# Block-sparse attention and a gated product in one kernel: attention steps of 512 tokens instead of 256, the probabilities' detour through DRAM in nine transfers instead of eighteen, and the first unit transposed on TensorE

## The chip, the cores and the metric

The kernel runs on one core of a Trainium2 chip. That core has five engines with queues of their own: TensorE (PE, with its weight loads as PEld), VectorE (DVE), ScalarE (ACT), GpSimd (POOL) and SyncE (SP), which here only issues DMA transfers. Each engine works its queue strictly in order. The metric is the device time of one execution in microseconds (us).

## The reference: what is computed

Four sequences of 768 tokens go through attention with 8 heads of 64, and the result, 3072 tokens of 512, goes through a gated product.

```python
scores = scale * np.matmul(q, k.transpose(0, 1, 3, 2))
is_global = pos[None, :] < int(n_global)
is_local = (rel >= 0) & (rel < int(n_local))
keep = is_global | is_local
...
scores = scores + bias[None, :, :, :]
scores = np.where(keep, scores, -1000000000.0)
...
a = a / (np.sum(a, axis=-1, keepdims=True) + 1e-09)
return np.matmul(a, v).astype(np.float32)
...
a = x @ w_a
b = x @ w_b
return (a * b @ w_out).astype(np.float32)
```

A query sees the first 8 tokens and the 96 up to itself. The bias is a slope per head times the distance. The product's hidden size is 1536. All is float32.

## The kernel before

**Units and passes.** The 3072 tokens are six units of 512 (T, L38). The hidden columns are six groups of 256, two of which make a stage. `PASSES` (L47) names 18 passes: stage 0 over units 0 to 5, stage 1 back from 5 to 0, stage 2 from 0 to 5. A pass projects one unit's tokens with two groups (`project`, L811, whose seven products of 12 matmuls are L797 and go to the PSUM banks al and ga) and multiplies the gated result into four accumulators (`back`, L885, matmuls at L895, banks acc). Each float32 matmul is three of rounded parts: tokens (`forms`, L728) and weights (`wform`, L382) are split into a high part H and a low part L by a cast (L291 on ScalarE, L293 on VectorE) and a subtraction (L301). The seven products are a scheme of sums and differences, so that B11, T2 and the others are combinations of quarters of x, and A11, S2 and the others of quarters of the weights. A weight comes as 64-bit words (L322, 512 KB each) and is converted in steps on ScalarE (L328, L363) and VectorE (L335 to L370).

**Attention** of a unit must be done before its first pass. Unit 0's stands ahead of everything; the attention of unit u + 1 is spread over the second half of pass u - 1 or so and the first half of pass u. It is done in granules: one head pair (of four) and 256 tokens (NH = 2 blocks of 128), eight to a unit (`granule_ops`, L518).

- Loads: q in two transfers, one a head, into a buffer whose other half GpSimd set to zero once (L502), so that one matmul gives both heads' scores; keys kt and values vt, one transfer each.
- Scores: two matmuls a block (L555), of 168 columns each, for 64 queries of both heads and 168 keys. VectorE adds the mask and takes the maximum (L570), ScalarE does exp and the sum (L586), VectorE the reciprocal (L600, L605). The scaling of the granule goes to ScalarE in four instructions (L611) or to VectorE in one (L614), as the planner finds it.
- Turning: the values matmul needs the probabilities with the keys on the partitions. VectorE transposes blocks of 32 x 32 into tt (L624, L631). Four transfers write tt to a mirror in DRAM, mir, by 32 partitions each (L639). Five read it back with the blocks' rows in place: three into px (keys near the query block, and 8 lanes of global keys for each half), two into py (the others).
- Values: eight matmuls (L693) into the bank pa, half of a pair's 512 tokens. After the second granule pa is copied to x (L711).

**The order.** Nothing runs as it is written. Each step is recorded with a due time and a cost for each engine that may do it (`Schedule`, L121). A planner plays them through with those costs, lets the earliest due ready step go first, and writes out one fixed order per engine. A DMA counts as bytes / 330 ns, 90 ns at least, on one queue (L285). All transfers are issued by SyncE, in the planner's order: when one has to wait for a semaphore, all behind it wait. Buffers are tags with a number of copies (`TBUFS` and so on, L57 to L64); a step waits for a free copy. x takes two copies of a tag X, shared with the tokens that later passes load again (`load_x`, L776).

Of the kernel before, what the change touches and what calls it, by code (L numbers as in the profile page):

```python
# [12 lines left out]
F32 = mybir.dt.float32  # L13
# [12 lines left out]
P = 128  # L26
# [9 lines left out]
KB = KW + 72  # L36
# [6 lines left out]
NH = 2  # L43
# [22 lines left out]
AHEAD = 0.5  # L66
START = 44000.0
# [186 lines left out]
class Fast:  # L254
    def __init__(self, ctx, tc, a, out, nf):
        self.tc, self.nc = tc, tc.nc
        self.a, self.out, self.nf = a, out, nf
        self.ctx = ctx
        self.plan = Schedule()
        self.count = 0  # L260
        self.granule = 0

# [16 lines left out]
    def dma(self, due, out, src, reads, writes, nbytes):  # L279
        self.plan.op(  # L280
            due,
            lambda e: self.nc.sync.dma_start(out(), src()),  # L282
            reads,
            writes,
            dma=max(nbytes / 330.0, 90.0),  # L285
        )
# [23 lines left out]
    def to32(self, fp, piece, due, tag):  # L310
# [13 lines left out]
            dma=CN * 8 * P / 330.0,  # L324
# [67 lines left out]
    def convert(self, fp, due, step, direct):  # L392
# [19 lines left out]
        temp("S2", m["S1"], m["A11"], sub, t)  # L412
        self.wform(fp, "S2", t, m["S2"], direct)
        self.wform(fp, "S1", t + 200, m["S1"], direct)
        temp("S3", m["A11"], m["A21"], sub, t + 400, out=m["A21"])
# [4 lines left out]
        for f in range(2):  # L420
            w = self.to32(fp, 4 + f, due + (4 + f) * step, "mO")
            self.wform(fp, f"O{f}", due + (4 + f) * step, w, direct)
# [68 lines left out]
    def zeros(self):  # L491
        self.q = [self.sbuf([P, NH * 2, 2, 64], F32, f"q{i}", f"q{i}") for i in range(QBUFS)]
        self.px = [
            self.sbuf([104, 4, 2, NH, 32], F32, f"px{i}", f"px{i}") for i in range(PTBUFS)
        ]
        self.py = [self.sbuf([P, 4, 2, NH, 32], F32, f"py{i}", f"py{i}") for i in range(PTBUFS)]
        for q in self.q:
            for h in range(2):
                r = slice(64 * (1 - h), 64 * (1 - h) + 64)
                self.plan.op(  # L500
                    -1e6,
                    lambda e, q=q, r=r, h=h: self.nc.gpsimd.memset(q[r, :, h], 0.0),  # L502
                    [],
                    [(q, "z%d" % h)],
                    pool=400,
                )
# [11 lines left out]
    def granule_ops(self, u, p, hb, due, x):  # L518
        nc, op = self.nc, self.plan.op
        n = f"{u}_{p}_{hb}"  # L520
        g = self.granule
        self.granule += 1
        q, px, py = self.q[g % QBUFS], self.px[g % PTBUFS], self.py[g % PTBUFS]
        kt = self.sbuf([P, KN], F32, "kt", "kt" + n, KBUFS)
        vt = self.sbuf([P, VN], F32, "vt", "vt" + n, VBUFS)
        for h in range(2):
            r = slice(64 * h, 64 * h + 64)
            self.dma(
                due - LOADLEAD,
                lambda r=r, h=h: q[r, :, h],  # L530
                lambda h=h: self.a["qd"][u, p, hb, h].rearrange("d (s i) -> d s i", i=64),
                [],
                [(q, h)],
                64 * 1024,
            )
# [3 lines left out]
        self.dma(  # L539
            due + VLAG - 4000.0, lambda: vt[:, :], lambda: self.a["vd"][u, p, hb], [], [vt], VN * 4 * P  # L540
        )
        t = self.sbuf([P, NH, 2 * KW], F32, "t", "t" + n, TBUFS)
        sm = self.sbuf([P, 4, 2 * NH], F32, "sm", "sm" + n, 4)
        qreads = [(q, 0), (q, 1), (q, "z0"), (q, "z1")]
        for i in range(NH):
            blk = (4 * u + NH * hb + i) % NB
# [5 lines left out]
            def scores(e, i=i, ps=ps):  # L552
                for s in range(2):
                    k0 = i * KB + 72 * s
                    nc.tensor.matmul(  # L555
                        ps[:, s * KW : s * KW + KW],
                        q[:, 2 * i + s].rearrange("p h i -> p (h i)"),
                        kt[:, k0 : k0 + KW],
                        start=True,
                        stop=True,  # L560
                        skip_group_check=True,
                    )

            op(due, scores, qreads + [kt], [ps], pe=620)
# [33 lines left out]
        op(  # L598
            due,
            lambda e: nc.vector.tensor_scalar_add(sm[:, 2], sm[:, 1], 1e-9),  # L600
            [(sm, j) for j in range(4)],
            [(sm, "d")],
            dve=70,
        )
        op(due, lambda e: nc.vector.reciprocal(sm[:, 3], sm[:, 2]), [(sm, "d")], [(sm, "r")], dve=80)  # L605
        flat = lambda: t[:, :].rearrange("p a b -> p (a b)").rearrange("p (j k) -> p j k", k=KW)

        def norm(e):
            if e == "act":
                for j in range(2 * NH):  # L610
                    nc.scalar.mul(flat()[:, j], flat()[:, j], sm[:, 3, j : j + 1])  # L611
            else:
                r = sm[:, 3].rearrange("p (j o) -> p j o", o=1).to_broadcast([P, 2 * NH, KW])
                nc.vector.tensor_mul(flat(), flat(), r)  # L614

        ts = [(t, j) for j in range(4)]
        op(due, norm, [(sm, "r")], ts, port=BOTH, dve=dve(2 * NH * KW), act=4 * (act(KW) + 100))
        tt = self.sbuf([P, 2, 3, 2 * NH * 32], F32, "tt", "tt" + n, TTBUFS)

        def turn_x(e):  # L620
            src = t[:, :, 72:264].rearrange("p b (s e k) -> p b s e k", s=2, e=3)
            dst = tt[:, 0].rearrange("p e (s b k) -> p b s e k", b=NH, s=2)
            for i in range(NH):
                nc.vector.transpose(dst[:, i], src[:, i])  # L624

        def turn_y(e):
            for s in range(2):
                c = s * (2 * KW - 96)
                src = t[:, :, c : c + 96].rearrange("p b (e k) -> p b e k", e=3)
                dst = tt[:, 1].rearrange("p e (s b k) -> p s b e k", b=NH, s=2)  # L630
                nc.vector.transpose(dst[:, s], src)  # L631

        op(due, turn_x, ts, [(tt, 0)], dve=2 * dve(192))
        op(due, turn_y, ts, [(tt, 1)], dve=2 * dve(192))
        mir = self.dram([4, 2, 3, 32, P], F32, "mir" + n, "mir", 4)
        for k in range(4):
            self.dma(
                due,
                lambda k=k: mir[k].rearrange("a e j c -> j (a e) c"),  # L639
                lambda k=k: tt[32 * k : 32 * k + 32].rearrange("p a e c -> p (a e) c"),  # L640
                [(tt, 0), (tt, 1)],
                [(mir, k)],
                32 * 6 * 512 * 1.3,
            )
        ms = [(mir, k) for k in range(4)]

        def read(out, src, nbytes, writes):
            self.dma(due, out, src, ms, writes, nbytes)

        read(  # L650
            lambda: px[:96].rearrange("p g s b k -> p g (s b k)"),
            lambda: mir[:, 0].rearrange("g e j c -> (e j) g c"),
            96 * 4 * 512 * 1.3,
            [(px, "x")],
        )
        y = lambda: mir[:, 1].rearrange("g e j (s b k) -> s (e j) g b k", s=2, b=NH)
        read(
            lambda: py[:64, :, 0].rearrange("p g b k -> p g (b k)"),
            lambda: y()[0, :64].rearrange("p g b k -> p g (b k)"),
            64 * 4 * 256 * 2,  # L660
            [(py, 0)],
        )
        read(
            lambda: py[64:, :, 1].rearrange("p g b k -> p g (b k)"),
            lambda: y()[1, 32:96].rearrange("p g b k -> p g (b k)"),
            64 * 4 * 256 * 2,
            [(py, 1)],
        )
        for s, e0 in ((0, 64), (1, 24)):
            read(  # L670
                lambda s=s: px[96:104, :, s].rearrange("p g b k -> p g (b k)"),
                lambda s=s, e0=e0: y()[s, e0 : e0 + 8].rearrange("p g b k -> p g (b k)"),
                8 * 4 * 512,
                [(px, ("g", s))],
            )
        if hb == 0:
            tag = "psA" if u else FIRST["psA"][p % 2]
            self.pa = self.bank(tag, f"pa{u}_{p}")
        pa = self.pa

        def values(e):
            for i in range(NH):
                c0 = (NH * hb + i) * P
                v0 = i * 2 * P
                for c in range(2):
                    for h in range(2):
                        if c == 0:
                            rhs = px[:, 2 * h : 2 * h + 2, :, i].rearrange("p g s k -> p s g k")
                            lhs = vt[:104, v0 + 64 * h : v0 + 64 * h + 64]
                        else:  # L690
                            rhs = py[:, 2 * h : 2 * h + 2, :, i].rearrange("p g s k -> p s g k")
                            lhs = vt[:, v0 + P + 64 * h : v0 + P + 64 * h + 64]
                        nc.tensor.matmul(  # L693
                            pa[64 * h : 64 * h + 64, c0 : c0 + P],
                            lhs,
                            rhs,
# [6 lines left out]
        op(  # L703
            due + VLAG,
            values,
# [668 lines left out]
```

## Time and profile before

| what | us |
|---|---|
| median of three runs | 853.27 (852.32 to 854.04) |
| the profiled execution | 850.4 |
| its span, first to last instruction | 848.6 |
| TensorE busy in the span | 724.2 |
| VectorE busy | 580.0 |
| ScalarE busy | 378.1 |

The profile's page gives busy times, a chain of waits that ended last, and groups of instructions; the trace behind it can be asked for stretches of time. SPq is SyncE issuing transfers. A busy engine isn't one at its peak: matmuls overlap, and TensorE's clock is lowered at times (PEclk, 1.00 is full speed). DMA is the mean busy share of 16 transfer engines. In lists, names are line, engine, operation, and tiles as out<-in with buffer numbers left out; a time in a row's middle is the group's busy time, then the mean of one in ns.

### The profile page before, as it was taken

The numbers are of one execution on the slowest core, as the hardware profiler recorded it, in microseconds if no ns is written. First come the engines' busy times: TensorE is split into PE (matmuls) and PEld (weight loads), VectorE is DVE, ScalarE is ACT, GpSimd is POOL, SyncE is SP. The second block draws the span as 40 slices with busy tenths as digits, with TensorE's granted clock in tenths as the row PEclk, the third lists the DMA queues.
The fourth block names the chain that finished last, engine by engine and source line by source line (L and its number), as shares of the span: only waits on it lengthen the run. The fifth ranks groups of instructions, "written<-read, shape, count | busy, mean of one in ns | idle before, by whom it ended". The sixth has DMA issues, their size and how long they took to land.

```text
span 848.6 us, 14458 instructions
## 1 busy us (share of the span) xinstructions
PE 724.2 (85%) x5040; PEld 652.2 (77%) x5040; DVE 580.0 (68%) x1534; ACT 378.1 (45%) x952; POOL 2.7 (0%) x12
## 2 busy tenths in 40 slices
PE   3645778788888787888869999999999999999995
PEld 3544666577777576777669999999999999999994
DVE  5746977766668386477669988856765856765642
ACT  2644765735556464465446654323323322322320
POOL 1000000000000000000000000000000000000000
PEclk9855888789999999889979999999999999999998
DMA  6769688778878878889897666322353322420331
GB/s 191 193 162 280 203 206 221 209 186 227 219 198 238 251 225 217 202 229 241 240 333 240 215 225 222 121 91 99 131 162 101 102 80 73 149 88 13 100 100 66
DMA packets 162369, 149.60 MB, mean 176 GB/s; under 512 B 65392, under 2 KB 126832, under 8 KB 160240
## 3 DMA queue, kind: packets, MB, share of 16 engines
q1 hardware_dynamic: 162288, 148.59, 59.9%
q8 instruction: 42, 0.69, 0.3%
q14 instruction: 39, 0.32, 0.1%
HBM read 97.16 MB, written 51.38 MB: 175 GB/s over the span
## 4 chain that ended last, share of the span: by engine, by line
PE 57%; SPq 15%; DMA 13%; DVE 9%; issue 3%; ACT 2%; DVEq 0%; ACTq 0%
PE acc L895 19%; PE al L797 19%; SPq L282 14%; PE ga L797 14%; DMA px<-mir 4%; PE ps L555 3%; PE pa L693 2%; DMA wr<-wts 2%; DMA mir<-tt 2%; DMA kt<-kd 1%; DVE t L570 1%; ACT t L586 1%; DVE xT L301 1%; DVE s L826 1%; DVE tt L624 1%
## 5 line engine op out<-in xcount | busy, mean ns | idle before, releaser
L895 PE MATMUL acc<-w_O,hh 128*128 128x512 f32 x576 | 200.4, 407 | 0.9 <-ACT o L291 0.9
L895 PEld LDWEIGHTS acc<-w_O,hh 128*128 128x128 f32 x576 | 110.3, 192 | 25.3 <-ACT o L291 1.1
L555 PE MATMUL ps<-kt,q 128*128 128x168 f32 x384 | 88.4, 366 | 47.2 <-DMA kt<-kd 20.8
L797 PE MATMUL al<-xf_T,w_S 128*128 128x256 f32 x864 | 119.2, 288 | 5.9 <-ACT s L291 4.0
L797 PEld LDWEIGHTS al<-xf_T,w_S 128*128 128x128 f32 x864 | 111.2, 194 | 7.8 <-ACT s L291 4.8
L555 PEld LDWEIGHTS ps<-kt,q 128*128 128x128 f32 x384 | 69.7, 225 | 60.3 <-issue 24.4
L895 PE MATMUL acc<-w_O,hl 128*128 128x512 f32 x288 | 114.9, 399 | 0.5 <-DVE hl L301 0.5
L586 ACT ACTIVATE t<-t,sm 128x168 f32<-128x168 f32 x192 | 81.7, 427 | 71.3 <-DVE sm L570 65.9
L570 DVE CUSTOM_DVE_ANT_0 t<-ps,mask 128x168 f32<-128x168 f32 x192 | 57.0, 325 | 64.7 <-PE ps L555 64.3
L291 ACT COPY s<-al 128x512 f32<-128x512 f32 x70 | 41.0, 586 | 121.2 <-PE al L797 120.9
L693 PE MATMUL pa<-px,vt 104*64 104x128 f32 x384 | 47.1, 321 | 55.3 <-DMA px<-mir 32.8
L693 PEld LDWEIGHTS pa<-px,vt 104*64 104x64 f32 x384 | 27.0, 156 | 68.6 <-issue 31.0
L826 DVE TENSOR_TENSOR s<-ga,s 128x512 f32<-128x512 f32 x72 | 49.5, 688 | 39.0 <-PE ga L797 38.9
L291 ACT CAST hh<-h 128x512 fp32r<-128x512 f32 x62 | 38.2, 619 | 62.2 <-DVE h L301 36.5
L797 PE MATMUL ga<-xf_B,w_A 128*128 128x256 f32 x432 | 62.6, 295 | 2.6 <-DVE xf_B L301 1.5
L895 PEld LDWEIGHTS acc<-w_O,hl 128*128 128x128 f32 x288 | 55.3, 192 | 10.7 <-DVE hl L301 0.8
L797 PEld LDWEIGHTS ga<-xf_B,w_A 128*128 128x128 f32 x432 | 57.4, 200 | 4.3 <-DVE xf_B L301 2.3
L797 PE MATMUL ga<-xf_B,w_S 128*128 128x256 f32 x432 | 58.9, 286 | 1.7 <-ACT s L291 1.6
L797 PEld LDWEIGHTS al<-xf_B,w_A 128*128 128x128 f32 x432 | 57.6, 195 | 3.2 <-ACT t L611 0.3
L797 PE MATMUL al<-xf_B,w_A 128*128 128x256 f32 x432 | 59.8, 289 | 0.0
L797 PE MATMUL ga<-xf_T,w_S 128*128 128x256 f32 x432 | 57.9, 283 | 0.0
L797 PE MATMUL al<-xf_T,w_A 128*128 128x256 f32 x432 | 57.8, 283 | 0.1
(92 smaller groups left out, 1064.5 us busy)
## 6 DMA issues: line engine op xcount, KB each, us to landing
wr<-wts SPq DMA_DIRECT2D x36, 512.0 KB
mir<-tt SPq DMA_DIRECT2D x192, 96.0 KB
vt<-vd SPq DMA_DIRECT2D x48, 256.0 KB
kt<-kd SPq DMA_DIRECT2D x48, 240.0 KB
part<-o SPq DMA_DIRECT2D x40, 256.0 KB
xl<-dx SPq DMA_DIRECT2D x10, 1024.0 KB
o<-part SPq DMA_DIRECT2D x40, 256.0 KB
px<-mir SPq DMA_DIRECT2D x48, 192.0 KB
```

Of the source, the lines that this page charges most:

```text
L282: lambda e: self.nc.sync.dma_start(out(), src()),
L291: self.nc.scalar.copy(out(), src())
L301: lambda e: self.nc.vector.tensor_tensor(out(), a(), b(), op=op),
L555: nc.tensor.matmul(ps[:, s * KW : s * KW + KW], q[:, 2 * i + s].rearrange("p h i -> p (h i)"), kt[:, k0 : k0 + KW], start=True, stop=True, ...
L570: lambda e, i=i, w=w, ps=ps, j=j, kind=kind: nc.vector.tensor_tensor_reduce(t[:, i, w], ps[:, w], self.mask[p][:, kind, w], -0.125, 3.0e38 ...
L586: lambda e, i=i, w=w, j=j: nc.scalar.activation(t[:, i, w], t[:, i, w], AF.Exp, bias=sm[:, 0, j : j + 1], scale=-1.0, accum_out=sm[:, 1, j ...
L624: nc.vector.transpose(dst[:, i], src[:, i])
L693: nc.tensor.matmul(pa[64 * h : 64 * h + 64, c0 : c0 + P], lhs, rhs, start=c == 0, stop=c == 1, skip_group_check=True, tile_position=(0, 64 ...
L797: self.nc.tensor.matmul(bank[:, ab * HT : ab * HT + HT], w[:, a, (2 * ab + c) * P : (2 * ab + c) * P + P], x[:, b, c], start=first, stop=F ...
L826: lambda e: nc.vector.tensor_tensor(s[:, :], bank[:, :], s[:, :], op=ALU.add),
L895: self.nc.tensor.matmul(acc[i][:, :], a[:, rows], w[:, b], start=first and f == 0 and k == 0, stop=False, skip_group_check=True,)
```

## The change

A granule becomes one head pair and all 512 tokens of the unit (NH = 4). What follows from that and what is changed beside it:

- q and the keys come in one transfer, qk, of 7808 bytes for each of 128 partitions; q carries its zeros from DRAM. The keys are laid out once more, so that both halves of a block use overlapping windows (KB = KW + 64).
- Sums' reciprocals, scaling and transposes are done by halves of a granule (two blocks). On VectorE the scaling is four tensor_scalar instructions of 168 columns, no longer one multiplication with a broadcast.
- The mirror is written whole by one transfer, and read by eight: four into px of 32, 32, 32 and 8 partitions, four into py of 32 (`carry`).
- For unit 0 (`DIRECT`) there is no mirror. TensorE transposes each block's probabilities against an identity into PSUM (`direct`), and VectorE or ScalarE copies them to px and py. The identity is made ahead of the branch.
- px, py, tt and X have one copy each, K and V buffers two, temporaries s three. In bytes px, py, tt, t, qk and vt are twice as large as the granule's were.
- Due times of the start and the costs of the planner (DMA: bytes / 345, 340 ns at least, reads of the mirror at that least) are set anew, so the order shifts everywhere.

```diff
-KB = KW + 72
+KB = KW + 64
-NH = 2
+NH = 4
+QN = NH * 2 * P
...
+    "psT": ("acc3", "ga"),
...
-TTBUFS = 2
-PTBUFS = 2
-KBUFS = 3
-VBUFS = 3
-QBUFS = 2
-XBUFS = 2
+TTBUFS = 1
+PTBUFS = 1
+DIRECT = (0,)
+KBUFS = 2
+VBUFS = 2
+XBUFS = 1
...
-            dma=max(nbytes / 330.0, 90.0),
+            dma=max(nbytes / 345.0, 340.0),
...
         self.dma(
-            due - LOADLEAD, lambda: kt[:, :], lambda: self.a["kd"][u, p, hb], [], [kt], KN * 4 * P
+            due - LOADLEAD,
+            lambda: qk[:, :],
+            lambda: self.a["qk"][u, p],
+            [],
+            [qk],
+            (QN + KN) * 4 * P,
         )
...
-                r = sm[:, 3].rearrange("p (j o) -> p j o", o=1).to_broadcast([P, 2 * NH, KW])
-                nc.vector.tensor_mul(flat(), flat(), r)
+                    for j in js:
+                        nc.vector.tensor_scalar(
+                            flat()[:, j], flat()[:, j], sm[:, 3, j : j + 1], None, op0=ALU.mult
+                        )
...
+            if u in DIRECT:
+                for i in range(2 * half, 2 * half + 2):
+                    self.direct(u, n, i, due, t, px, py)
+                continue
...
+    def direct(self, u, n, i, due, t, px, py):
...
+        def turn(e):
+            for s in range(2):
+                x0, y0 = 64 + 104 * s, 272 * s
+                nc.tensor.transpose(
+                    bank[:104, s * P : s * P + P], t[:, i, x0 : x0 + 104], self.ident
+                )
+                nc.tensor.transpose(
+                    bank[:64, 256 + s * P : 256 + s * P + P], t[:, i, y0 : y0 + 64], self.ident
+                )
...
+    def carry(self, n, due, tt, px, py):
+        mir = self.dram([P, 6, 2 * NH * 32], F32, "mir" + n, "mir", 4)
+        self.dma(
+            due, lambda: mir[:, :], lambda: tt[:, :], [(tt, 0), (tt, 1)], [mir], 6 * 1024 * P
+        )
+        turned = lambda: mir[:, :].rearrange("(g j) e c -> j g e c", g=4)
+        for e in range(4):
+            lanes = 32 if e < 3 else NG
...
+                lambda e=e, lanes=lanes: turned()[:lanes, :, e],
+                [mir],
+                [(px, e)],
+                0,
+            )
...
-        temps = [self.sbuf([P, T], F32, "s", f"s{n}_{k}", 4) for k in range(3)]
+        temps = [self.sbuf([P, T], F32, "s", f"s{n}_{k}", 3) for k in range(3)]
...
-        x0 = self.attention(0, 0.0, START - 9000.0)
-        self.convert(0, START - 14000.0, 3000.0, True)
+        x0 = self.attention(0, 0.0, START - ATT0)
+        self.convert(0, START - CONV0, STEP0, True)
```

SyncE's queue before, at the first head pair of unit 1 (the digits after a name are unit, pair and granule half; 32x6x128 is partitions by runs by elements):

```order
L282 DMA mir1_0_0_807<-tt1_0_0_780 32x6x128 x4
L282 DMA q1_106<-qd 64x4x64 x2
L282 DMA kt1_2_0_838<-kd 128x480
L282 DMA px0_264<-mir1_0_0_807 96x4x128
L282 DMA py0_109<-mir1_0_0_807 64x4x64 x2
L282 DMA px0_264<-mir1_0_0_807 8x4x64 x2
L322 DMA wr1_2_872<-wts 128x512
L282 DMA mir1_0_1_881<-tt1_0_1_866 32x6x128 x4
L282 DMA q0_101<-qd 64x4x64 x2
L282 DMA kt1_2_1_911<-kd 128x480
L322 DMA wr1_3_935<-wts 128x512
L282 DMA px1_328<-mir1_0_1_881 96x4x128
```

The same place in SyncE's queue now:

```order
L290 DMA mir1_0_765<-tt1_0_720 128x1536
L330 DMA wr1_1_792<-wts 128x512
L290 DMA px0_214<-mir1_0_765 32x4x256 x3
L290 DMA px0_214<-mir1_0_765 8x4x256
L290 DMA py0_106<-mir1_0_765 32x4x128 x4
L290 DMA qk1_3_853<-qk 128x1952
L290 DMA vt1_2_911<-vd 128x1024
L290 DMA mir1_1_922<-tt1_1_843 128x1536
```

The write of the whole pair is one row and its reads eight issues; where the second granule's write and reads followed, the next pair's loads and its mirror stand.

TensorE's queue before, between the first and the second group of values matmuls of unit 0 (ps scores, pa values):

```order
L693 MATMUL pa0_0_304<-py0_109,vt0_0_0_132 64x128 x2
L555 MATMUL ps0_2_1_1_324<-kt0_2_1_206,q1_106 128x168 x2
L555 MATMUL ps0_3_0_0_331<-kt0_3_0_290,q0_101 128x168 x2
L555 MATMUL ps0_3_0_1_363<-kt0_3_0_290,q0_101 128x168 x2
L693 MATMUL pa0_0_304<-px1_328,vt0_0_1_137 64x128 x2
```

TensorE's queue now, at the same scores of unit 0's third pair (pt are the transposes; the two rows of a 64-query half have 104 and 64 columns of keys):

```order
L676 MATMUL pt0_0_3_228<-ident_60,t0_0_141 64x128
L544 MATMUL ps0_2_0_239<-qk0_2_166 128x168 x2
L544 MATMUL ps0_2_1_250<-qk0_2_166 128x168 x2
L673 MATMUL pt0_1_0_260<-ident_60,t0_1_169 104x128
L676 MATMUL pt0_1_0_260<-ident_60,t0_1_169 64x128
```

Four transposes a block now stand on TensorE in unit 0, where only scores and values stood, and a pair's values come in one group behind them.

More of the change, by code (lines that the diff above doesn't have):

```diff
@@ L261, in __init__ @@
         self.granule = 0
+        self.turns = 0
     def open(self):
@@ L645, in granule_ops @@
[L645 to L662, printed above, removed]
@@ L718, in granule_ops @@
                 psum=True,
             )
+    def carry(self, n, due, tt, px, py):
[6 more added lines that the diff above has]
+            lanes = 32 if e < 3 else NG
+            self.dma(
+                due,
+                lambda e=e, lanes=lanes: px[32 * e : 32 * e + lanes].rearrange(
+                    "p g s b k -> p g (s b k)"
+                ),
+                lambda e=e, lanes=lanes: turned()[:lanes, :, e],
[3 more added lines that the diff above has]
+            )
+        half = NH * 32
+        for s in range(2):
+            for e in range(2):
+                r = slice(64 * s + 32 * e, 64 * s + 32 * e + 32)
+                self.dma(
+                    due,
+                    lambda r=r, s=s: py[r, :, s].rearrange("p g b k -> p g (b k)"),
+                    lambda s=s, e=e: turned()[:, :, 4 + e, s * half : s * half + half],
+                    [mir],
+                    [(py, (s, e))],
+                    0,
+                )
```

290 lines of the change are left out of this document (129 added, 161 removed).

## The prediction, made before any run of the changed kernel

> **What bounds the kernel now.** I read the busy shares by stretch first, then the chain that ended last, then the DMA queue's own timeline. I cut the span at two instructions. At 85 us TensorE begins the product of S2 and T2, the first for which the weights and tokens of the first pass are really there. At 432 us the last values matmul of unit 5 is over, and attention with it. I call the pieces A (0 to 85), B (85 to 432) and C (432 to 848.6).
>
> ```profile
> core 0: us, PE busy (x) PEld busy (x) DVE busy (x) ACT busy (x) POOL busy (x), PEclk, DMA share, GB/s
> 0.00:85.00 85.00, 42.56 (x225) 36.36 (x226) 51.62 (x180) 38.10 (x115) 2.65 (x12) 0.72 0.75 206
> 85.00:432.00 347.00, 277.19 (x2022) 240.67 (x2021) 240.97 (x831) 194.95 (x582) 0.00 (x0) 0.92 0.82 222
> 432.00:520.00 88.00, 86.03 (x601) 80.63 (x601) 80.29 (x153) 50.85 (x93) 0.00 (x0) 0.97 0.74 249
> 520.00:840.00 320.00, 318.46 (x2197) 294.56 (x2195) 206.43 (x372) 94.18 (x165) 0.00 (x0) 1.00 0.31 102
> L797 PE MATMUL al<-xf_T,w_S x864: 276/280/582, 84.9 to 824.2; 128*128 128x256 f32 x173
> 428.33 1.99 PE pa L693 x16
> ```
>
> In C TensorE is busy throughout, at the full granted clock: 416.6 us that no DMA edit can shorten. In B it is busy for 277 us at a granted clock of 0.92, which is 277 x 0.92 = 255 us of work at full clock in 347 us. So 92 us of B are loss, and most of A is. The chain of waits, taken for B alone, says to what:
>
> ```profile
> by line: SPq L282 29.1%; DMA px<-mir 10.9%; PE ps L555 5.3%; PE pa L693 5.2%; issue 5.1%; PE acc L895 5.1%; DMA mir<-tt 4.5%; PE al L797 3.2%; DMA wr<-wts 2.9%; DMA kt<-kd 2.5%; DVE t L570 2.4%; PE ga L797 1.7%; ACT t L586 1.7%; DVE s L826
> ```
>
> The largest entry is neither a transfer nor an engine, but SyncE issuing transfers (SPq). Its timeline in B shows why: it issues without a pause.
>
> ```profile
> 276.20 0.32 SPq L282 DMA_DIRECT2D px<-mir  x1
> 276.58 1.26 SPq L282 DMA_DIRECT2D py<-mir  x2
> 277.88 0.85 SPq L282 DMA_DIRECT2D px<-mir  x2
> 278.83 0.34 SPq L282 DMA_DIRECT2D part<-o  x1
> 279.22 1.23 SPq L282 DMA_DIRECT2D q<-qd  x2
> 280.50 0.60 SPq L282 DMA_DIRECT2D kt<-kd  x1
> 281.21 2.11 SPq L282 DMA_DIRECT2D mir<-tt  x4
> 283.37 0.47 SPq L322 DMA_DIRECT2D wr<-wts  x1
> 283.89 0.44 SPq L282 DMA_DIRECT2D vt<-vd  x1
> ```
>
> From 276.20 to 284.33 the issues alone fill 7.62 of 8.13 us. Now per head pair and 512 tokens (two granules): q 4 x 0.61, kt 2 x 0.60, vt 2 x 0.44, mir 8 x 0.53, px 2 x 0.32, py 4 x 0.63, the small px 4 x 0.43 = 13.6 us. Some twenty pairs lie in B, 272 us of its 347. The 20 pairs' 26 issues each are what sets B's pace, with the DMA engines at 0.82 close behind.
>
> **What the change does to the queue.** A pair now issues one qk, one vt, one mirror write and eight reads, 11 in place of 26. None of these shapes is in the trace. The rows above lie between 0.32 (px) and 0.63 (py), so 11 issues cost between 3.5 and 6.9 us. I take 0.45, near wr and vt: 5.0 us, 100 us in B. SyncE stops being the bound, with room to spare at either end. What is late next has to be found among the engines.
>
> **DMA bytes in B.** The sizes now:
>
> ```profile
> mir<-tt SPq DMA_DIRECT2D x192, 96.0 KB
> vt<-vd SPq DMA_DIRECT2D x48, 256.0 KB
> kt<-kd SPq DMA_DIRECT2D x48, 240.0 KB
> px<-mir SPq DMA_DIRECT2D x48, 192.0 KB
> q<-qd SPq DMA_DIRECT2D x96, 64.0 KB
> py<-mir SPq DMA_DIRECT2D x96, 64.0 KB
> px<-mir SPq DMA_DIRECT2D x96, 8.0 KB
> DMA packets 162369, 149.60 MB, mean 176 GB/s; under 512 B 65392, under 2 KB 126832, under 8 KB 160240
> ```
>
> A pair moves 8 x 96 + 2 x 256 + 2 x 240 + 2 x 192 + 4 x 64 + 4 x 64 + 4 x 8 = 2688 KB. After: qk 976 (the zeros that GpSimd wrote into q are now loaded), vt 512, mirror 768, reads 3 x 128 + 32 + 4 x 64 = 672, together 2928 KB. So the bytes grow by 240 KB a pair; only the packets shrink in number. B moves 347 x 222 = 77 MB now and 77 + 20 x 0.246 = 82 MB then. What a byte costs depends on the packet, and the stretches show it: divided by their share, B carries 222 / 0.82 = 271 GB/s, the next two stretches 249 / 0.74 = 336 and 102 / 0.31 = 329. They move rows of 2 KB and more, B mostly pieces of 256 and 512 B. The new qk, vt and mirror write are rows of 4 to 8 KB, the reads are still 512 B and 1 KB. So I price the 20 x 0.69 = 14 MB of reads at 271 and the other 68 MB at 333: 51 + 204 = 255 us of DMA time, against 0.82 x 347 = 285 now. At the present rate for all of it, it would be 82 / 271 = 303.
>
> **VectorE and TensorE in B.**
>
> ```profile
> L624 DVE STREAM_TRANSPOSE tt<-t 128x192 f32<-128x192 f32 x96 | 30.8, 357 | 8.2 <-DMA mir<-tt 6.7 <-ACT t L586 0.8 <-ACT t L611 0.5
> L631 DVE STREAM_TRANSPOSE tt<-t 128x192 f32<-128x192 f32 x96 | 28.6, 337 | 0.0
> L614 DVE TENSOR_TENSOR t<-t,sm 128x672 f32<-128x672 f32 x15 | 12.8, 856 | 0.2
> L335 DVE TENSOR_SCALAR wm<-wm 128x512 f32<-128x512 f32 x36 | 15.3, 424 | 25.9 <-ACT wm L328 25.9
> L600 DVE TENSOR_SCALAR sm<-sm 128x4 f32<-128x4 f32 x48 | 7.9, 165 | 7.5 <-ACT t L586 7.3
> ```
>
> A pair's transposes stay eight instructions over 1536 columns in all (4 x 256 + 4 x 128 for 8 x 192): no change. The scaling becomes four tensor_scalar of 168 columns for a half. That shape isn't in the trace; it lies between 165 and 424 ns, and I take 200, by its length. VectorE gets 31 of the 48 halves, some 96 such instructions in B: 19 us for about 12 x 0.856 = 10. VectorE goes from 241 to 250 us, and to 271 were it 424. TensorE keeps its 255 us. Thus three engines have 250 to 255 us of work each in B, and the pace depends on how well they overlap. From 432 to 520 us TensorE is busy 0.98 of the time with VectorE at 0.91; B now reaches 255 / 347 = 0.73. B keeps its round trips through memory, in a fixed order on every engine, so I take 0.86: 255 / 0.86 = **296 us**. Ends: 264 (0.97) and 347.
>
> **A.** The first unit no longer writes or reads the mirror: its four pairs lose 18 of their 26 issues and 1440 KB each. In their place stand 64 TensorE transposes, off the bound since TensorE is busy half of A, and copies out of PSUM.
>
> ```profile
> 9.46 0.57 DVE L468 TENSOR_SCALAR tab<-tab,nf 128x672 f32<-128x672 f32 x1 [4.92 <-DMA tab<-pos]
> L291 ACT COPY sa<-al 128x256 f32<-128x256 f32 x26 | 9.6, 369 | 23.7 <-PE al L797 20.5 <-DVE h L301 3.1
> ```
>
> VectorE loses 32 transposes of 0.347 (11 us) and gains 10 copies below 0.42 (3 us) and some 3 us of scaling: 51.6 becomes 46. It starts at 9.5 and is busy 51.6 / 75.5 = 0.68 now, because the mirror's trips starve it. At 0.80, between that and the 0.91 of the later stretch, A ends at 9.5 + 46 / 0.80 = **67 us**. ScalarE gains 38 copies of at most 0.37 (14 us) and gives up some 20 scalings: about 44 us of work from 15 us on, so A isn't below 59. The upper end is 85, no gain. The identity is made on GpSimd while the token counts are loaded, and GpSimd waits for them anyway.
>
> **C** I leave at 416.6. One X buffer for two means that a 1 MB load starts only when the pass before has formed its operands. A pass lasts 31 us and that load 1.05 / 0.249 = 4 us, which hides it; without that cover ten loads would cost 40 us.
>
> **The sum.** 67 + 296 + 416.6 = 779.6 us of span for 848.6. The profiled execution took 850.4, so 1.8 lie around the span, and the median of the runs is 853.27, 2.9 above it. 779.6 + 1.8 + 2.9 = **784 us**.
>
> **Rivals.**
>
> 1. *The relief is hidden: a byte costs what it costs now.* Then the DMA engines have 303 us of work in B, and at 0.86 that takes 352; with A at 67 the total is 840. Against it stand the 329 to 336 GB/s of later stretches, for it that the reads stay small. 0.07.
>
> 2. *The eight reads are slow because each fills 32 lanes or fewer.* At half rate 0.69 MB take 5.1 us for 2.5, over 20 pairs 51 us more: 306 / 0.86 = 356 and a total of 844. In the trace most of B's transfers already go to or from 32, 64 or 96 lanes (the mirror's writes, py), and B still carries 271 of 333 GB/s for a full share, which speaks against a halving; no transfer on 32 lanes runs alone there. The Trainium skill, SBUF — State Buffer, section "Door 1: The DMA port swizzle", states this rule: 32 partitions reach 8 of 16 ports, hence about half the bandwidth. Its figures, 189 GB/s for 32 partitions and 328 for 128, would price the reads at an estimated 3.6 us a pair. 0.06.
>
> 3. *One px and py for two: slower.* SyncE may issue a pair's reads only when the values of the pair before are done, and the next loads stand behind it on the queue.
>
> ```profile
> 113.28 6.42 DMA px<-mir
> 346.17 5.38 DMA px<-mir
> 501.79 5.61 PE acc L895 x24
> ```
>
> Eight issues take 3.6, the last read lands within 5.4 to 6.4, the values of four blocks take up to 2 x 1.99: at most 14 us, against 296 / 20 = 14.8 a pair. If the values also wait behind a whole back step of 5.6 on TensorE, the cycle is 19.6 and B 392: 67 + 392 + 416.6 + 4.7 = 880. It turns slower than before from (853.3 - 67 - 416.6 - 4.7) / 20 = 18.3 us a pair. Against it: the old cycle of two granules already fits 17.4, and landings are long now because the queue is full. 0.07.
>
> **How the numbers follow.** The forecast, 745 to 815, has 0.73; below 745 (A 59, B 264) 0.05; rivals 0.07, 0.06 and 0.07; no change 0.02. A measurement tells 0.2% (1.7 us) from no change. Faster by more: 0.73 + 0.05 + 0.07 + 0.06 = 0.91; same 0.02; slower 0.07. The range 745 to 842 leaves out 0.05 below, and above it rivals 2 and 3: 0.18.
>
> **What would show it.** Right: SPq falls from 29% of B's chain to under 10%; the product of S2 and T2 starts near 67 and attention ends near 363; the DMA share in B is 0.8 to 0.9 at over 310 GB/s for a full share; the stretch behind attention keeps 416 us. Wrong in the bytes: a rate near 271. Wrong in the lanes: px and py landings of over 6 us with a DMA share below 0.8. Wrong in the buffers: SyncE or TensorE waiting at the values matmul for px in most pairs, with more than 18 us between two pairs. The forecast fails as a whole if C grows, or if A stays near 85.

## The result, and the profile after

The changed kernel takes 772.26 us (median of four runs, 769.55 to 777.12), the kernel before 853.65 (852.32 to 854.65): a ratio of 0.9054, interval 0.8998 to 0.9109. The forecast was 784, range 745 to 842. The profiled execution is the slowest of the four, 777.12 us, with a span of 775.3.

The span is cut at the same two instructions as before, found in the list of the product's line and in TensorE's timeline at the end of attention (start, duration):

```profile
L809 PE MATMUL al<-xf_T,w_S x864: 276/280/582, 64.2 to 748.5; 128*128 128x256 f32 x173
```

```profile
352.83 0.42 PE L648 MATMUL pa<-py,vt 128*64 128x128 f32 x4
```

So A is 64 us (85 before), B 289 (347) and C 422 (416.6). By stretches:

```profile
core 0: us, PE busy (x) PEld busy (x) DVE busy (x) ACT busy (x) POOL busy (x), PEclk, DMA share, GB/s
0.00:64.00 64.00, 36.72 (x296) 31.08 (x296) 48.28 (x196) 41.29 (x138) 1.75 (x8) 0.94 0.64 236
64.00:353.00 289.00, 257.43 (x2012) 227.27 (x2012) 243.98 (x897) 181.86 (x538) 0.00 (x0) 0.97 0.85 274
353.00:440.00 87.00, 82.38 (x582) 76.60 (x579) 77.53 (x146) 48.80 (x87) 0.00 (x0) 0.98 0.66 229
440.00:760.00 320.00, 320.00 (x2211) 296.45 (x2210) 206.44 (x371) 100.06 (x175) 0.00 (x0) 1.00 0.31 106
```

Three readings. B carries 289 x 274 = 79 MB at 274 / 0.85 = 322 GB/s for a full share, where it was 271; its DMA time is 0.85 x 289 = 246 us (0.82 x 347 = 285 before). TensorE's work in B is 257 x 0.97 = 250 us at full clock, that is 0.86 of B. And C is 5.7 us longer than before: behind attention, at 353 to 440, TensorE misses 4.6 us (2.0 in the like stretch before), and 12.4 us lie behind TensorE's last instruction (10.2 before). That is this one execution: in a run of the same kernel with one load cut differently (qk_cols below), C is 770.7 - 353.5 = 417 us.

The chain of waits in B no longer has SyncE's issuing (SPq) in front; it was 29.1% and is 4.5%:

```profile
by line: DMA mir<-tt 17.5%; DMA wr<-wts 10.8%; DMA qk<-qk 9.4%; PE pa L648 7.3%; PE al L809 6.9%; PE ps L544 5.5%; DVE tt L634 5.3%; PE acc L907 5.1%; SPq L290 4.5%; PE ga L809 3.9%; DVE t L559 3.7%; DMA py<-mir 3.7%; issue 2.4%; DVE t L615
```

What stands in front is the mirror's write landing. SyncE's issues in B, by tile (count, then least, median and longest in ns), and what SyncE waited for there (us, times, longest):

```profile
L290 SPq DMA_DIRECT2D px<-mir x80: 318/422/1443, 78.5 to 347.6; - x80
L290 SPq DMA_DIRECT2D py<-mir x80: 302/430/966, 80.2 to 349.3; - x80
L290 SPq DMA_DIRECT2D mir<-tt x20: 320/377/819, 75.2 to 340.2; - x20
L290 SPq DMA_DIRECT2D qk<-qk x17: 327/377/1546, 82.3 to 309.3; - x17
```

```profile
SPq L290 <- DMA mir<-tt: 57.6, 18, 6.2
SPq L290 <- PE pa L648: 18.6, 9, 5.5
SPq L330 <- DVE wm L378: 14.1, 4, 8.2
SPq L290 <- DMA qk<-qk: 12.8, 6, 2.8
```

All issues in B add up to 124 us where they were 282, and SyncE's waits to 166 where they were 45. At 18 of 20 mirror writes SyncE now stands still until the write has landed, 57.6 us in all. In B of the kernel before the same wait was a tenth:

```profile
SPq L282 <- DMA mir<-tt: 5.3, 11, 0.8
```

So which counted, the issues themselves or the trip that the mirror makes through one in-order queue? That SyncE's issuing set B's pace has this rival: B is paced by a serial trip for each granule through SyncE's queue (turn, write issued, landed, reads issued, landed, values), 40 trips in B before, 20 after. Further rivals are bytes, packet sizes and lanes.

### The profile page after: what moved, and what is told of

Its sections match the earlier page's. It is cut to its first block, busy times and chain, and to the rows that moved or that the text cites. A ratio compares the mean times of both kernels' runs of the same rounds, so it can differ in the third digit from the quotient of the medians.

```text
span 775.3 us, 13998 instructions
## 1 busy us (share of the span) xinstructions
PE 699.4 (90%) x5104; PEld 633.3 (82%) x5104; DVE 579.0 (75%) x1610; ACT 372.0 (48%) x937; POOL 1.7 (0%) x8
## 4 chain that ended last, share of the span: by engine, by line
PE 61%; DMA 19%; DVE 13%; ACT 3%; SPq 2%; issue 2%; DVEq 0%; ACTq 0%
PE al L809 20%; PE acc L907 20%; PE ga L809 15%; DMA mir<-tt 7%; DMA wr<-wts 5%; DMA qk<-qk 4%; PE pa L648 3%; PE ps L544 3%; DVE tt L634 2%; SPq L290 2%; DVE t L559 2%; DMA py<-mir 1%; ACT t L575 1%; DVE t L615 1%; DVE xf_T L309 1%
## 5 line engine op out<-in xcount | busy, mean ns | idle before, releaser
L907 PE MATMUL acc<-w_O,hh 128*128 128x512 f32 x576 | 197.9, 403 | 0.0
L907 PEld LDWEIGHTS acc<-w_O,hh 128*128 128x128 f32 x576 | 108.5, 188 | 23.1 <-issue 0.3
L544 PE MATMUL ps<-qk 128*128 128x168 f32 x384 | 76.6, 329 | 28.5 <-DMA qk<-qk 18.3
L544 PEld LDWEIGHTS ps<-qk 128*128 128x128 f32 x384 | 60.4, 199 | 38.3 <-DVE sm L559 15.0
L809 PE MATMUL ga<-xf_B,w_A 128*128 128x256 f32 x432 | 59.8, 288 | 4.7 <-ACT xf_B L299 2.6
L809 PEld LDWEIGHTS ga<-xf_B,w_A 128*128 128x128 f32 x432 | 55.2, 192 | 5.8 <-ACT xf_B L299 3.1
L809 PEld LDWEIGHTS ga<-xf_B,w_S 128*128 128x128 f32 x432 | 53.6, 188 | 3.4 <-ACT s L299 3.1
L809 PEld LDWEIGHTS al<-xf_T,w_A 128*128 128x128 f32 x432 | 54.4, 188 | 2.4 <-DVE s L838 1.4
```

The lines of the kernel that those rows point to most:

```text
L544: nc.tensor.matmul(ps[:, s * KW : s * KW + KW], qk[:, (2 * i + s) * P : (2 * i + s) * P + P], qk[:, k0 : k0 + KW], start=True, stop=True, ...
L809: self.nc.tensor.matmul(bank[:, ab * HT : ab * HT + HT], w[:, a, (2 * ab + c) * P : (2 * ab + c) * P + P], x[:, b, c], start=first, stop=F ...
L907: self.nc.tensor.matmul(acc[i][:, :], a[:, rows], w[:, b], start=first and f == 0 and k == 0, stop=False, skip_group_check=True,)
```

## The experiments

In the table, "issues" is the sum of SyncE's issue instructions in B, "wait" SyncE's wait for the mirror's write there, "DMA" the DMA share times B; all in us, from each run's trace. The time is the median. Mean times of packets of one size, below, are those of B's packets in each trace.

| run | time | A | B | issues | wait | DMA |
|---|---|---|---|---|---|---|
| before | 853.65 | 85 | 347 | 282 | 5 | 285 |
| after | 772.26 | 64 | 289 | 124 | 58 | 246 |
| pieces26 | 865.55 | 72 | 373 | 245 | 12 | 306 |
| pieces44 | 1013.14 | 72 | 523 | 397 | 7 | 287 |
| extra15 | 946.00 | 68 | 455 | 312 | 30 | 332 |
| small_packets | 786.35 | 66 | 298 | 151 | 48 | 274 |
| qk_rows | 790.98 | 71 | 300 | 148 | 48 | 273 |
| qk_cols | 771.31 | 64 | 289 | 147 | 44 | 249 |
| no_direct | 776.77 | 76 | 281 | 120 | 67 | 242 |
| before_pool | 850.32 | 89 | 345 | 200 | 70 | 273 |
| pool_stale | 825.49 | 83 | 318 | 201 | 0 | 280 |
| before_reads_pool | 870.05 | 87 | 364 | 187 | 1 | 276 |
| after_reads_pool | 816.34 | 63 | 335 | 51 | 0 | 248 |
| two_px | 822.78 | 58 | 300 | 128 | 49 | 255 |

**More issues, same bytes.** Two kernels cut the changed kernel's transfers back into 26 and 44 issues a pair, the order on TensorE, VectorE and ScalarE unchanged. In pieces26:

```diff
-            lambda: qk[:, :],
-            lambda: self.a["qk"][u, p],
...
+                (lambda r=part(4, i): qk[r, :], lambda r=part(4, i): self.a["qk"][u, p, r])
+                for i in range(4)
...
+                (lambda r=part(8, i): mir[r], lambda r=part(8, i): tt[r])
+                for i in range(8)
```

vt goes in two pieces and each py read in two. In pieces44 qk, vt and the mirror write go in four pieces each and each of the eight reads in four.

> The changed kernel with the same bytes, the same contiguous runs and the same order on TensorE, VectorE and ScalarE, but 26 issues a pair again for 11: qk in 4 parts, vt in 2, the mirror's write in 8 (all by partitions), the py reads in 2 each. My theory, that SyncE's issuing paced the stretch of attention (B) before: 26 issues of about 0.42 us and the gaps between them make 12.5 us a pair, 250 us for twenty pairs and 305 with the other transfers, so B grows from 289 to 310 to 330 us and the time to 795 to 815. Rival, that packet size alone was the gain: within 1% of the changed kernel's 772.

> As the run with 26 issues, with 44 issues a pair (qk, vt and the mirror's write in 4 parts each, every read in 4 parts). Theory: 44 x 0.42 us with gaps is 21 us a pair, 420 us for twenty and 475 with the others, which B cannot be shorter than: over 940 us in all. Rival of packet size: about 772, as the runs are as long as before.

pieces26 took 865.55, a ratio to before of 1.0120 (1.0091 to 1.0149); pieces44 1013.14, 1.1846 (1.1807 to 1.1884). Their stretches B, and the start of pieces44's chain in B:

```profile
71.70:444.75 373.05, 291.90 (x2012) 254.16 (x2012) 245.80 (x897) 182.15 (x537) 0.00 (x0) 0.89 0.82 215
```

```profile
71.60:594.30 522.70, 329.47 (x2012) 278.82 (x2012) 245.29 (x897) 182.72 (x537) 0.00 (x0) 0.76 0.55 153
```

```profile
by line: SPq L299 44.7%; DMA qk<-qk 9.2%; DMA wr<-wts 8.1%; PE pa L663 6.6%; issue 6.5%; DMA mir<-tt 5.7%; DMA py<-mir 3.2%; DMA dx<-x 2.9%; DMA px<-mir 2.0%; PE ps L559 1.5%; PE acc L938 1.3%; SPq L290 1.3%; DMA wl_A<-dw_A 1.3%; PE al L840
```

In pieces44, which took over 940 as expected, issuing is the largest part of B's chain by far, with the DMA engines half idle (0.55). pieces26 came out 50 us above what I expected, and the sum of its issues does not explain it: it issues less than the kernel before (245 us for 282), yet its B is 26 us longer, and in its chain DMA px<-mir (17.4%) stands ahead of SyncE's issuing (15.8%). Its pieces are also narrow, 16 to 64 lanes, so it moves two things at once. The next kernels take these by themselves.

**More issues, hardly any bytes.** extra15 adds 15 transfers of 64 bytes, DRAM to DRAM, to the 11 of a pair: three behind qk, two behind vt, two behind the mirror's write and one behind each read.

```diff
+            for _ in range(more):
...
+                x = self.dr.tile([16, 1], F32, tag=f"no{self.tiny}", name=f"no{self.tiny}")
+                self.nc.sync.dma_start(x[:, :], self.a["pos"][:16, 0:1])
```

> The changed kernel, same transfers and same order, with 15 transfers a pair added on SyncE that move 64 bytes each from DRAM to DRAM and that nothing waits for: 26 issues a pair. Theory of issuing: the run with 26 issues in partition pieces also made transfers narrower, and its TensorE-free share of DMA rose to 306 us of work, so its 373 us of B were two things. Here the bytes cost nothing; 15 x 0.35 to 0.42 us a pair are 105 to 126 us more for SyncE in B, whose own issues take 155 of 289 now and about 110 more are waits, so B is 310 to 345 and the time 793 to 830. Rival, that the earlier loss came from narrow transfers alone: within 1% of 772.

946.00 us, 1.1100 (1.1052 to 1.1148), far above what was expected.

```profile
67.70:523.00 455.30, 305.08 (x2012) 269.02 (x2012) 245.75 (x898) 182.56 (x537) 0.00 (x0) 0.79 0.73 176
```

```profile
L293 SPq DMA_DIRECT2D no<-pos x287: 488/495/2125, 78.8 to 515.2; - x144
```

The 287 issues in B add up to 166 us, and B grew by 166. That the two are equal is partly chance. SyncE's waits in B did fall, from 166 to 118 us (58 to 30 for the mirror's write), but the other issues got longer by 22 us in all (146 for 124), and some 25 us of SyncE's B are neither an issue nor a wait that the trace shows (none in the changed kernel). So what the waits gave was lost again elsewhere. The added transfers also did more than occupy SyncE: a 512-byte packet took 69 ns on the mean for 36 and a 4 KB one 259 for 195, and the DMA time rose by 86 us. Ten of the fifteen stand in the trip, behind the mirror's write and the reads, and five behind loads; the run doesn't part them. It shows that added issues cost B about their own length, not that SyncE's time alone is the reason.

**Lanes alone.** The qk load in four transfers, by 32 partitions each (qk_rows) or by 488 columns of all 128 partitions (qk_cols). Issues and bytes are the same.

```diff
+                (lambda i=i: qk[32 * i : 32 * i + 32, :], lambda i=i: self.a["qk"][u, p, 32 * i : 32 * i + 32, :])
```

```diff
+                (lambda i=i: qk[:, 488 * i : 488 * i + 488], lambda i=i: self.a["qk"][u, p, :, 488 * i : 488 * i + 488])
```

> The changed kernel with qk in four transfers of 32 partitions, each run still 7808 bytes: 14 issues a pair. If a transfer to 32 partitions is slow by itself, qk's runs take 1.5 times as long as whole (as they did in the run with 26 issues, 538 ns for 375), which adds 22 us of work for the transfer engines in B and makes the time 785 to 800. If only issues count, 3 more cost at most 25 us of a queue that has room: 772 to 780, the same as with columns.

> The changed kernel with qk in four transfers of 488 columns on all 128 partitions, runs of 1952 bytes: also 14 issues a pair. Theory of partitions: within 1% of 772, since runs of 2 KB cost hardly more by the byte. Theory of run length: slower by as much as the run with small pieces everywhere (786).

790.98 us (789.01 to 792.22), ratio 0.9271 (0.9229 to 0.9313), against 771.31 (767.84 to 774.46), ratio 0.9042 (0.8989 to 0.9094), both as the theory of partitions had it. First qk_rows' B, then qk_cols':

```profile
71.00:371.20 300.20, 262.96 (x2012) 231.16 (x2012) 244.05 (x896) 182.30 (x537) 0.00 (x0) 0.96 0.91 265
```

```profile
64.10:353.50 289.40, 261.57 (x2012) 232.32 (x2012) 244.17 (x898) 181.91 (x537) 0.00 (x0) 0.95 0.86 275
```

Three more issues for a load cost nothing that shows (289.4 for 289): SyncE's issues in B grow by 23 us, and its waits shrink from 166 to 137, at the mirror's write from 58 to 44. 32 lanes cost 20 us (11 in B, 7 in A): a 7808-byte packet takes 526 ns on the mean where the changed kernel's takes 375. The Trainium skill, SBUF — State Buffer, section "Door 1: The DMA port swizzle", states that 32 partitions reach half the ports. The direction agrees; here the packet takes 1.4 times as long, not twice.

**Packet sizes alone.** small_packets moves qk, vt and the mirror's write in runs of 488, 512 and 1024 bytes instead of 4 to 8 KB, with the same 11 issues and lanes.

```diff
-            lambda: qk[:, :],
-            lambda: self.a["qk"][u, p],
+            lambda: qk[:, :].rearrange("p (a c) -> p a c", a=16),
+            lambda: self.a["qk"][u, p].rearrange("a p c -> p a c"),
```

> The changed kernel with its 11 issues a pair and the same order, but small runs: qk lies in DRAM in 16 parts of 488 bytes a partition, vt in 8 of 512, the mirror in 6 of 1 KB. Theory: SyncE has room, so issuing does not matter; the transfer engines, at 0.85 of B's 289 us (246 us of work), get about 3.2 us more a pair, 64 us in B. At the share of 0.85 to 0.93 B is 333 to 365 and the time 815 to 850. Rival, that the number of issues is all that counts: within 1% of 772.

786.35 us, 0.9190 (0.9157 to 0.9222): between the two expectations, and far below that of the theory.

```profile
65.80:364.00 298.20, 262.96 (x2012) 233.55 (x2012) 244.20 (x897) 182.21 (x537) 0.00 (x0) 0.95 0.92 267
```

The rate for a full share falls to 267 / 0.92 = 290 GB/s and the DMA time rises by 28 us, of which 14 reach the end (9 of them in B). That is what runs of this size cost, of 81 us won; the runs of 256 bytes that the kernel before also had were not put back.

**The first unit alone.** no_direct lets unit 0 go through the mirror like the others.

```diff
-DIRECT = (0,)
+DIRECT = ()
```

> The changed kernel with unit 0 on the mirror's path like the others (no TensorE transposes). Theory: the first unit's trips through DRAM delay the first full products from 64 us to about 80, so 785 to 792 us. Rival, that the weights' conversion sets the start: no change (770 to 776).

776.77 us (773.91 to 779.04), 0.9071 (0.9039 to 0.9103): below what was expected, and just above its rival's range.

```profile
0.00:76.50 76.50, 40.29 (x249) 33.87 (x249) 58.75 (x244) 40.36 (x130) 1.75 (x8) 0.82 0.82 274
76.50:357.40 280.90, 254.90 (x1996) 229.55 (x1996) 233.66 (x840) 182.85 (x537) 0.00 (x0) 0.95 0.86 283
```

A is 12 us longer without the TensorE transposes, and B 8 us shorter. The VectorE columns go with that: some 10 us of its work stand in A instead of B (58.75 for 48.28, and 233.66 for 243.98). The transposes bring some 4.5 us of the 81, and as the ranges of the two kernels' runs overlap, even that is not sure.

**Fewer issues on SyncE, in the kernel before, in the same order.** In before_pool the loads of q, kt and vt, 8 of 26 issues, are issued by GpSimd.

```diff
-            lambda e: self.nc.sync.dma_start(out(), src()),
+            lambda e: queue.dma_start(out(), src()),
...
+                pool=True,
```

> The kernel before, same order and same transfers, with the loads of q, keys and values issued by GpSimd, which does nothing else: SyncE keeps 18 of 26 issues a pair. Theory of issuing: SyncE saves 4.5 us a pair, 90 us in B, and what is left is the transfer engines' 285 us at 0.85 to 0.95: B 300 to 335 for 347, the time 806 to 842. Rival, that the number and size of packets bound B before: within 1% of 854.

850.32 us, 0.9955 (0.9927 to 0.9984). SyncE issues 82 us less in B, and B is 2 us shorter, which the issues' theory did not allow. Its issuing falls from 29.1% of B's chain to 12.0% without B following. The same bytes also go in fewer packets by the trace (90182 in B for 113786, 77 MB in each), and the DMA time is 12 us less, so that two things at once bring next to nothing. The reason is in SyncE's waits:

```profile
88.60:433.80 345.20, 279.74 (x2022) 244.52 (x2020) 241.90 (x830) 193.05 (x578) 87.74 (x148) 0.90 0.79 222
```

```profile
SPq L283 <- DMA mir<-tt: 69.8, 68, 4.0
SPq L283 <- DVE sm L572: 18.7, 9, 5.4
```

Of the 82 us freed, 65 are spent waiting for the mirror's write (70 us for 5). The loads' issues had lain under its landing. The Trainium skill, Perfetto Trace Analysis, section "DMA Optimizations", says that spreading transfers over issuing engines may help where descriptor generation is the bottleneck; SyncE's queue looked like that case, and it brought 0.45%.

To test this, pool_stale is before_pool with each granule's reads taken from the mirror of the granule before, which landed long ago. It leaves out the wait for the granule's own write, and so computes something else; issues, bytes and order are the same.

```diff
+        old, self.old = getattr(self, "old", mir), mir
...
-            lambda: mir[:, 0].rearrange("g e j c -> (e j) g c"),
+            lambda: old[:, 0].rearrange("g e j c -> (e j) g c"),
```

> The kernel before with its loads issued by GpSimd (as in the run before_pool, 850.3), in which the five reads of a granule moreover fetch the mirror of the granule before, which landed long ago: the outputs are then not the reference's, but issues, bytes, packets and the order on every engine are the same; only the wait for the mirror's landing is gone (69.8 us at the head of SyncE's queue in before_pool). Theory (B is paced by the serial trip of each granule, turn, write, landing, read, values, in which the landing stood as much as the issues): B falls from 345 to 285-315, the time to 790-820. Rival (the landing ran beside work that is long anyway; packets or the values matmuls set B): 840-852.

825.49 us (822.84 to 830.05), 0.9671 (0.9608 to 0.9733).

```profile
82.72:400.59 317.87, 272.62 (x2021) 238.71 (x2020) 240.47 (x828) 191.69 (x578) 87.62 (x147) 0.93 0.88 239
```

```profile
SPq L283 <- DVE sm L572: 36.2, 17, 7.2
SPq L283 <- DVE tt L633: 14.0, 6, 6.5
SPq L283 <- DMA px<-mir: 10.5, 15, 3.3
SPq L283 <- DMA py<-mir: 6.4, 8, 1.8
SPq L283 <- DMA mir<-tt: 0.2, 1, 0.2
```

B is 27 us shorter, with not one issue less. It is 5 us outside the trip's expectation and 15 outside its rival's: the landing did pace B, once the loads' issues no longer covered it, though less than I gave it. Of 70 us of waiting, about 27 were time; SyncE now waits longer for the softmax and the turning (sm, tt) and for reads, with the DMA engines 0.88 busy. Older data read with the loads still on SyncE was not tried, so what the landing is worth in the kernel before, where SyncE waited 5 us for it, stays open.

**The reads on another queue.** GpSimd issues the mirror's reads, in the kernel before (before_reads_pool, 200 issues) and in the changed one (after_reads_pool, 160). In the latter, each read's call ends in the new argument:

```diff
+        queue = self.nc.gpsimd if pool else self.nc.sync
...
                 0,
+                True,
```

> The kernel before, with the five mirror reads of each granule (200 of its 520 attention transfers) issued by GpSimd instead of SyncE; the order of TensorE, VectorE and ScalarE is as before. Theory now (B is paced by one serial trip for each granule through SyncE's queue: mirror written, landed, read, landed, with the loads of the next granules behind them): SyncE no longer stands before a read, and its issues in B fall from 282 to about 182 us, so B shrinks from 347 to 290-320 and the time to 795-825. Rival (the bytes and the DMA engines' packets set B, whoever issues): 845-855, as with the loads on GpSimd.

> The kernel after, with the eight mirror reads of each pair issued by GpSimd; order of the other engines unchanged. SyncE waited 57.6 us for the mirror's landing and 18.6 for the values in B. If these waits at the head of SyncE's queue still hold B above TensorE's 257 us, B falls from 289 to 265-280 and the time to 748-763. Rival (DMA engines at 0.85 share set B): within 1% of 772. Second rival (a GpSimd issue costs more than SyncE's, and all of it lies in the trip): 775-790.

Both are slower than their bases: 870.05, a ratio to before of 1.0143 (1.0090 to 1.0196), and 816.34, 0.9534 (0.9510 to 0.9558), where the changed kernel has 0.9054. No expectation held. The read's landing after its issue (the last column, median us of the landings that the trace tells), in after_reads_pool and, for the same read issued by SyncE, in qk_cols, then the chain of after_reads_pool's B:

```profile
py<-mir POOLq DMA_DIRECT2D x80, 64.0 KB, 5.2
```

```profile
py<-mir SPq DMA_DIRECT2D x80, 64.0 KB, 3.3
```

```profile
by line: DMA py<-mir 21.3%; PE pa L649 14.2%; POOL px L291 8.1%; PE al L812 8.0%; issue 7.2%; POOL py L291 6.4%; PE ps L545 6.2%; DMA mir<-tt 5.7%; PE acc L910 5.4%; PE ga L812 4.0%; DVE tt L635 2.2%; DVE t L560 2.1%; DVE s L841 1.2%; DVE t
```

The eight reads of a pair take GpSimd 89 / 20 = 4.5 us to issue (SyncE 67 / 20 = 3.4): 1.1 us for each of 20 pairs, 22 us, where B grew by 46 (to 335). Whether they also land later is not shown: the trace tells all 80 of GpSimd's landings but only 13 of SyncE's 80, and for the 128 KB reads into px the medians are 4.8 from GpSimd (60 of 60 told) and 5.1 from SyncE (7 of 60). Were the 1.9 us by which py's rows differ right for the last read, it would be 3.0 us a pair, 60 us. Either way the trip gets longer instead of being relieved. So these two runs don't test what the head of SyncE's queue costs; they fit a B that follows the trip, and don't prove it.

**Two copies of px and py.** two_px pays for them with one buffer of w for two, and two for three of hh, hl and o; this also changes the planner's order.

```diff
-PTBUFS = 1
+PTBUFS = 2
...
-WSBUFS = 2
+WSBUFS = 1
```

> The kernel after with two buffers each of px and py (paid for by one buffer of w instead of two and fewer small buffers of the hi and lo forms and of o). If the wait of the mirror's reads for the values matmuls of the pair before (18.6 us of SyncE's time in B, and the only work that one px holds back) counts, B shrinks by 5-18 us: 755-767. If it is hidden behind the other transfers: 768-777. If the missing buffers elsewhere cost something: above 777.

822.78 us, 0.9596 (0.9563 to 0.9629), the last of the three cases expected. Its B and C:

```profile
57.90:358.00 300.10, 267.29 (x2020) 236.29 (x2020) 252.19 (x919) 183.97 (x544) 0.00 (x0) 0.93 0.85 275
358.00:825.00 467.00, 425.67 (x2797) 389.12 (x2796) 290.10 (x515) 149.76 (x264) 0.00 (x0) 0.93 0.35 116
```

B isn't shorter with two copies (300 for 289), and C, which has no attention, is 467 us, 45 more: the missing buffers, or the new order, cost that. With that much else changed, it doesn't settle what the one px costs.

## Why the prediction was right, point by point

**The sum, 784.** 772. Of the 12 us between them only 4 lie in the span (775.3 for 779.6). The rest is the step from the profiled execution to the median: it was 2.9 us below the median before, and I added that; now it is 4.9 above.

**C, 416.6.** 422 in the profiled execution, 417 in qk_cols. In kernels with the order from before it is 417 to 420 (before, before_pool, pool_stale). Loading x later cost nothing that shows.

**A, 67.** 64. VectorE has 48 us of work in A for the 46 forecast, and from its start at 9.8 us it is busy 0.89 of the time, where I had 0.80. The cause is split otherwise: no_direct shows that A falls from 85 to 76 without any transposes on TensorE, and the other 12 us come from them but are mostly given back in B. I counted none of that return.

**The issues' price.** I took 5.0 us a pair, 100 us in B. The five kinds of issue of a pair add up to 93 us in B (px 35, py 32, qk 10, mirror 8, vt 7). Before, a pair's kinds take 256 us in B, where 8 us of the timeline had given me 272; and over all of B SyncE did pause, for 45 us.

**The DMA engines, 255 us at 0.86.** 246 us. 322 GB/s for a full share, against 82 MB / 255 us = 322 forecast. small_packets shows that this rate hangs on the packets' size, and that the size alone moves the total by 14 us.

**B, 296.** 289, since TensorE's 250 us (255 forecast) fill 0.86 of it, the overlap that I had chosen. That choice was an estimate between two neighbours, and that it was met so closely is luck, no proof of the reason. VectorE has 244 us of work in B for 250, though its scaling instruction took 303 ns on the mean where I took 200.

**The step that failed is the reason given for B's pace**: "The 20 pairs' 26 issues each are what sets B's pace". Taking 8 of the 26 away brought 0.45% (before_pool), and a kernel with 245 us of issues for 282 was slower (pieces26). What the runs show in its place: SyncE's queue is one station of a serial trip. Issues added all along the queue cost about their own length (extra15, which slows other packets too), a load's issue doesn't count while the mirror's landing covers it (before_pool, qk_cols), and the landing counts once no issue covers it (pool_stale). B before took 347 / 40 = 8.7 us a trip; now it is 289 / 20 = 14.5 us for one with twice the tokens. The forecast could stand on the wrong reason because the change does both: fewer issues, and half the trips. How B's 58 us divide between the halved trips, the issues and the 39 us less DMA time was not separated. In small_packets and qk_rows 28 and 27 us of DMA time made B 9 and 11 us longer; at that rate the 39 would be worth some 15, an estimate. pool_stale, the nearest to a kernel before without these waits, still has 318, with 280 us of DMA time.

**"SyncE stops being the bound, with room to spare"** is half right too: its issues leave the chain, but at its head it still stands 57.6 us for the landing.

**Rival 1** (a byte costs what it did, 0.07) fell by the 322 GB/s. **Rival 2** (lanes, 0.06): the effect is real, its price wasn't. qk_rows puts 24 loads of 1.0 MB on 32 lanes and loses 20 us, 0.8 us each; the eight reads of a pair move two thirds as much. What they would cost on more lanes was not tried. **Rival 3** (one px, 0.07): SyncE waited 18.6 us for the values in B, in 9 of 20 pairs, and a pair takes 14.5 us, well below the 18.3 from which it decides.

**The chances.** The range 745 to 842 leaves out "no change" (853) too, so 0.20 lay above it and not 0.18.

## What to carry to other kernels

A queue that issues nearly without a pause is not yet the bound: look for what its issues cover, and ask what it would wait for if they were gone. Where data make a round trip through memory on one in-order queue, count the trips and what lies in each (issue, landing, issue, landing); make the trips fewer and larger before spreading transfers over other engines. If a transfer has to be cut, cut it by columns over all partitions, not by rows (here 771 for 791 us, with runs of 2 KB).

## What was not expected of the hardware

- An issue on SyncE hardly depends on the bytes: in the changed kernel 0.35 us (median) for 512 KB of vt and 0.43 for a 64 KB read, in extra15 0.495 for 64 bytes. 287 of the latter slowed other packets too (512 bytes: 36 to 69 ns on the mean), though they moved 18 KB in all.
- 32 lanes: 526 ns for a 7808-byte packet where 128 lanes take 375.
- The issue of a mirror read takes GpSimd 0.55 us (median) and SyncE 0.42 to 0.43. The same q load of 64 KB landed 3.2 us after its issue from GpSimd (before_pool) and 3.0 from SyncE (before_reads_pool), all 74 told in each.
